# A spectral filter and a two-way maxout layer: filter loads in another order, and the first batch's input in fewer loads

## The chip, the cores and the metric

The kernel runs on one core of one Trainium2 chip. The metric is the device time of one execution in microseconds. A profile gives one execution's own span, from the first to the last instruction.

## The reference

```python
# x (8, 3072, 256), filt_r and filt_i (1537, 256); moe_w1 and moe_w2 (256, 1024), moe_w_out (1024, 256)
X = np.fft.rfft(x, axis=1)
Y = X * (filt_r + 1j * filt_i)[None, :, :]
y = np.fft.irfft(Y, n=3072, axis=1).astype(np.float32)
t = y.reshape(8 * 3072, 256)
out = np.maximum(t @ moe_w1, t @ moe_w2) @ moe_w_out
```

## The kernel before, in words

The transform of 3072 points is split into 96 by 32 points, and both steps and their inverses are matrix products on TensorE with bf16 tables of sines and cosines that the kernel makes at its start. The eight batches (indices 0 to 7) go through four steps one after another: a first transform over 96 points, a transform over 32 points (`s2`), the product with the filter (`product`, line 393), and the way back (`s3`, `s4`). The maxout layer works on 64 blocks of 384 tokens. Its matmuls (lines 453 and 481) make up most of the run, and an order written out by hand puts the transforms of batch b + 1 and b + 2 between the matmuls of batch b. Nothing of that can start before batch 0 has gone through its transforms, and batch 0 has code of its own: `s1t`, `t1`, `s2`, `products`, `s3t`, `t2`, in which the intermediate results stay on the core.

**What the start loads.** The program for GpSimd's queue begins with eight loads of x for batch 0, `load_x(0, c, 1)` for c from 0 to 7, with small index tables (`iota`) between the first ones. Each takes a chunk of 4 rows for each of 96 partitions, and the DMA turns float32 into bf16. `s1t(c)` on TensorE (line 507) transforms chunk c. Before it, 12 matmuls with no use for the result (`spin`, line 567) keep TensorE busy. Behind the x loads stand 18 loads of the filter.

**The filter's layout.** The filter tile `F` has 128 partitions, `[128, 2, 12, 2, 256]`: the second index `ri` is filt_r or filt_i, the third is `w` from 0 to 11. A load fills 16 partitions. Partitions fall into two array halves `g` (0 to 63 and 64 to 127). In each half, partitions 0 to 15 hold frequencies in rising order (the plus sign, line 121, one run of rows), partitions 16 to 31 hold frequencies in falling order (the minus sign, line 124, row by row backwards), and partitions 32 to 63 are a copy of the first 32. Where `g` is 0 and `w` starts at 0, the minus sign needs one more small load (line 127). `load_f(h, sign)` loads w 0 to 7 for h = 0 and w 8 to 11 for h = 1. So h = 0 has ten loads and h = 1 has eight.

**The copies.** `double_f(h, g, ri, engine)` copies partitions 0 to 31 of a half to 32 to 63, for four values of `w`. For w 4 to 7 (its h = 1) and 8 to 11 (h = 2) it is a DMA on SyncE's queue (line 136), eight in all; for w 0 to 3 (h = 0) it is a copy on VectorE (line 134). Each waits for the plus and the minus loads of its own `g` and `ri`. On SyncE, four loads of the layer's weights (lines 289 and 290) stand behind the eight copies.

**Who waits for the filter.** `products(v)` for v from 0 to 5 needs w 2v and 2v + 1 of both halves and of both `ri`: v 0 and 1 need VectorE's copies, v 2 and 3 SyncE's first four, v 4 and 5 its last four. For v below 4 one of its two products is on GpSimd, and all others are on VectorE. `s3t(v)` (lines 532 and 538) follows on TensorE.

**Semaphores.** The framework gives the DMAs of GpSimd's queue eight completion semaphores in turn. A DMA whose semaphore is still in use by the DMA eight places before it is issued only when that one has landed, and the queue behind it waits too.

Of the kernel before, what the change touches and what calls it, by code (L numbers as in the profile page):

```python
# [15 lines left out]
D = 256  # L16
# [10 lines left out]
def kernel(  # L27
# [15 lines left out]
    V, S, G, TE = nc.vector, nc.scalar, nc.gpsimd, nc.tensor  # L43
# [7 lines left out]
    F = const.tile([128, 2, NW, 2, D], BF16)  # L51
# [26 lines left out]
    def x_tile(b, c):  # L78
        if c % 2 == 0:
            xb[b] = xpool.tile([128, 8, D], BF16, tag="xb", name="xb")  # L80
        return xb[b][:, 4 * (c % 2):4 * (c % 2) + 4]

    def load_x(b, c, n):
        for k in range(c, c + n):
            xb[b, k] = x_tile(b, k)[0:NP]
        src = x[b].rearrange("(p m) d -> p m d", m=NM)
        m0 = 4 * (c % 2)
        G.dma_start(out=xb[b][0:NP, m0:m0 + 4 * n], in_=src[:, 4 * c:4 * c + 4 * n, :])  # L88
# [18 lines left out]

    WP = ((0, 8), (8, 12))

    def load_f(h, sign):  # L110
        w0, w1 = WP[h]
        n = 2 * (w1 - w0)
        for g in range(2):
            for ri, f in enumerate((filt_r, filt_i)):
                k0 = 24 * g + 2 * w0
                n0 = 1 if k0 == 0 else 0
                r0 = 64 * g if sign > 0 else 64 * g + 16
                o_ = F[r0:r0 + 16, ri, w0:w1].rearrange("p w s d -> p (w s) d")
                if sign > 0:
                    src = bass.AP(f.tensor, f.offset + k0 * D, [[96 * D, 16], [D, n], [1, D]])  # L120
                    G.dma_start(out=o_, in_=src)
                else:
                    src = bass.AP(f.tensor, f.offset + (96 - k0 - n0) * D, [[96 * D, 16], [-D, n - n0], [1, D]])
                    G.dma_start(out=o_[:, n0:n], in_=src)
                    if n0:
                        src = bass.AP(f.tensor, f.offset + 48 * D, [[96 * D, 16], [1, D]])
                        G.dma_start(out=o_[:, 0], in_=src)


    def double_f(h, g, ri, engine):  # L130
        ws = slice(4 * h, 4 * h + 4)
        o_, i_ = F[64 * g + 32:64 * g + 64, ri, ws], F[64 * g:64 * g + 32, ri, ws]
        if engine is V:
            V.tensor_copy(o_, i_)
        else:
            nc.sync.dma_start(out=o_, in_=i_)
# [3 lines left out]
    def load_fn():  # L140
        nc.sync.dma_start(out=FN[32:33], in_=filt_r[1536:1537, :])

    def fix_f():
        V.tensor_copy(F[32:33, 0, 0, 0], FN[32:33])
# [5 lines left out]
    def one(name):  # L150
# [11 lines left out]

    hv = init.tile([128, 2, 64], FP32)
    U0 = init.tile([128, 2, 64], BF16)
    load_x(0, 0, 1)
    G.iota(pid, pattern=[[1, 1]], base=0, channel_multiplier=1, allow_small_or_imprecise_dtypes=True)
    G.iota(kc.rearrange("p v g i s -> p v g (i s)"), pattern=[[4, 6], [24, 2], [1, 4]], base=0, channel_multiplier=0,
           allow_small_or_imprecise_dtypes=True)
    load_x(0, 1, 1)
    G.iota(kap, pattern=[[4, 6], [24, 2], [2, 2]], base=0, channel_multiplier=0,  # L170
           allow_small_or_imprecise_dtypes=True)
    G.iota(jb, pattern=[[1, 16]], base=0, channel_multiplier=0, allow_small_or_imprecise_dtypes=True)
    load_x(0, 2, 1)
    G.iota(cid, pattern=[[1, 128]], base=0, channel_multiplier=0, allow_small_or_imprecise_dtypes=True)
    for c in range(3, 8):
        load_x(0, c, 1)
    G.memset(hv, 1.0)
    for q in range(2):
        G.memset(hv[0:64, q, 0:64:32], 0.5 * (1 - q))
    for h in range(2):  # L180
        load_f(h, 1)
        load_f(h, -1)
    load_fn()

    def table_c():
# [329 lines left out]
    def t1(n, engine):  # L515
        pb = single.tile([128, 4, D], BF16, tag="single", name="pb")
        for i in range(4):
            for dc in range(2):
                TE.transpose(pb[:, i, 128 * dc:128 * dc + 128],
                             at2[:, dc, 4 * n + i].rearrange("p q m -> p (q m)"), I128)  # L520
        if engine is S:
            S.activation(bt[0][:, 4 * n:4 * n + 4], pb, AF.Copy)
        else:
            V.tensor_copy(bt[0][:, 4 * n:4 * n + 4], pb)
# [48 lines left out]
    V.tensor_scalar(NI, cid, pid, -1.0, OP.is_equal, OP.mult)  # L573
    tables_u()
    for h in (1, 2):
        for g in range(2):
            for ri in range(2):
                double_f(h, g, ri, nc.sync)
    for h in range(2):
        load_w(h)  # L580
# [10 lines left out]
    sines_u(1)  # L591
    for n in range(6):
        t1(n, S if n % 2 else V)
    for g in range(2):
        for ri in range(2):
            double_f(0, g, ri, V)
            if g == 0 and ri == 0:
                fix_f()
# [100 lines left out]
    for tt in range(8 * B + 1):  # L699
        b, i = divmod(tt, 8)  # L700
        k = 0
        for j in range(8):
# [5 lines left out]
            if tt > 0:  # L708
                n = 3 if j in (3, 7) else 4
# [36 lines left out]
```

## Time and profile before

| | us |
|---|---|
| median of 3 runs | 511.97 |
| lowest and highest run | 509.62, 512.15 |
| profiled execution, own time | 510.68 |
| its span | 508.9 |
| TensorE busy in the span | 492.5 (97%) |
| VectorE, ScalarE, GpSimd busy | 329.6, 307.6, 253.7 |

The profile's page groups instructions by line of the kernel; its other views are the chain of work that ended last, the timeline of one engine, sums over stretches of time, and the DMA issues with their time to landing. PE is TensorE, DVE VectorE, ACT ScalarE, POOL GpSimd, SP SyncE. A row of GpSimd's or SyncE's timeline named DMA_DIRECT2D is the issue of a transfer, not the transfer.

### The profile page before, as it was taken

The page shows a single profiled execution, that of the slowest core. Times are in us where ns is not written, and L with a number is a line of the kernel's source. Part 1 is how long each engine was busy: PE and PEld are TensorE (multiplying, and loading weights), DVE is VectorE, ACT ScalarE, POOL GpSimd, SP SyncE. Part 2 cuts the span into 40 slices and gives each one's busy share as a digit, 9 for nine tenths or more (in the row PEclk, how much of TensorE's full clock was granted, in tenths as well). Part 3 has the DMA queues.
Part 4 walks back from the last instruction along what each step waited for, and adds up shares of the span by engine and source line. Part 5 has one row for each costly group of instructions (what it writes and reads, how often), then busy time and mean ns, then how long its engine had stood idle before and what let it go on. Part 6 is the DMA issues. An engine that isn't in the chain of part 4 may idle for free.

```text
span 508.9 us, 13067 instructions
## 1 busy us (share of the span) xinstructions
PE 492.5 (97%) x5302; PEld 364.7 (72%) x5302; DVE 329.6 (65%) x517; ACT 307.6 (60%) x612; POOL 253.7 (50%) x334
## 2 busy tenths in 40 slices
PE   8679999999999999999999999999999999999996
PEld 4445777777777777777777777777777777777775
DVE  7655579656874677557774677657774687554453
ACT  6745558746784576646774576646774465544442
POOL 7783159674845566538636556538642221222220
PEclk9957999999999999999999999999999999999999
DMA  8998697999699778795689768797769326411112
GB/s 134 149 255 160 187 258 234 275 271 237 221 256 263 186 219 234 233 258 174 194 227 266 196 211 221 217 254 179 219 177 244 99 105 166 166 63 64 63 63 83
DMA packets 78158, 97.72 MB, mean 192 GB/s; under 512 B 8081, under 2 KB 54418, under 8 KB 78034
## 3 DMA queue, kind: packets, MB, share of 16 engines
q1 hardware_dynamic: 64834, 67.26, 50.3%
q0 software_dynamic: 13264, 29.64, 21.0%
q8 instruction: 41, 0.67, 0.6%
q14 instruction: 19, 0.16, 0.1%
HBM read 53.87 MB, written 47.19 MB: 199 GB/s over the span
## 4 chain that ended last, share of the span: by engine, by line
PE 90%; DMA 5%; DVE 2%; POOL 1%; issue 0%; SPq 0%; ACT 0%; DVEq 0%; POOLq 0%
PE po L481 34%; PE ph L453 32%; PE po L479 8%; PE pz L404 5%; PE py L433 4%; DMA F<-in_filt_r_dram 3%; PE pa L357 2%; PE px L387 2%; DMA xb<-in_x_dram 1%; DMA F<-F 1%; PE pr L557 1%; PE pz L538 1%; DVE at L335 0%; DVE pq L393 0%; PE pa L332 0%; POOL xb L88 0%
## 5 line engine op out<-in xcount | busy, mean ns | idle before, releaser
L481 PE MATMUL po<-Wo,gt 128*128 128x256 bf16 x1536 | 261.0, 273 | 0.0
L457 ACT ACTIVATE gt<-ph 128x384 bf16<-128x384 f32 x321 | 157.0, 496 | 148.1 <-PE ph L453 147.5
L481 PEld LDWEIGHTS <-gt 128*128 128x128 bf16 x1536 | 146.7, 98 | 65.7 <-issue 9.9
L466 POOL DMA_DIRECT2D out_dram<-ot x186 | 102.4, 555 | 179.5 <-DVE ot L493 176.7
L455 DVE TENSOR_SCALAR gt<-ph 128x384 bf16<-128x384 f32 x191 | 105.0, 553 | 62.9 <-PE ph L453 61.0
L393 DVE TENSOR_TENSOR pq<-px,F 128x1024 bf16<-128x1024 f32 x92 | 108.3, 1219 | 28.5 <-PE px L387 22.6
L453 PEld LDWEIGHTS <-Wd 128*128 128x128 bf16 x1024 | 96.6, 98 | 11.9 <-issue 0.5
L103 POOL TENSOR_TENSOR xb<-XF 128x512 bf16<-128x512 f32 x48 | 61.2, 1276 | 50.6 <-DMA XF<-in_x_dram 35.1
L493 DVE COPY ot<-po 128x512 f32<-128x512 f32 x95 | 65.2, 686 | 25.2 <-PE po L481 21.1
L104 POOL TENSOR_TENSOR xb<-XF 128x512 bf16<-128x512 f32 x48 | 61.0, 1272 | 0.0
L408 ACT ACTIVATE zt<-pz 128x512 bf16<-128x512 f32 x84 | 45.6, 595 | 11.5 <-PE pz L404 9.2
L361 ACT ACTIVATE at<-pa 128x512 bf16<-128x512 f32 x96 | 51.8, 610 | 1.2 <-PE pa L357 0.8
L433 PE MATMUL py<-G,zr 96*128 96x96 bf16 x512 | 32.9, 207 | 0.1
L433 PEld LDWEIGHTS <-zr 96*128 96x128 bf16 x512 | 29.3, 98 | 2.7 <-DVE zr L560 0.8
L387 PE MATMUL px<-bt,U 64*64 64x256 bf16 x384 | 20.6, 280 | 3.1 <-DVE pq L393 1.8
L404 PE MATMUL pz<-pq,VP 64*64 64x256 bf16 x336 | 21.9, 281 | 0.0
L404 PE MATMUL pz<-pq,VQ 64*64 64x256 bf16 x336 | 20.9, 269 | 0.0
L357 PE MATMUL pa<-xb,CT 64*64 64x512 bf16 x192 | 19.5, 383 | 0.0
L404 PEld LDWEIGHTS <-VP 64*64 64x64 bf16 x336 | 9.7, 105 | 13.3 <-issue 13.3
L387 PEld LDWEIGHTS <-U 64*64 64x64 bf16 x384 | 10.4, 108 | 6.6 <-issue 6.3
L567 PE MATMUL pd<-W 128*128 128x512 bf16 x31 | 12.0, 507 | 1.5 <-DVE zero L156 1.5
L560 DVE COPY zr<-pr 96x1024 bf16<-96x1024 bf16 (+1 forms) x8 | 5.2, 649 | 8.7 <-PE pr L557 8.7
(428 smaller groups left out, 607.6 us busy)
## 6 DMA issues: line engine op xcount, KB each, us to landing
out_dram<-ot POOLq DMA_DIRECT2D x186, 128.0 KB, 3.5
XF<-in_x_dram SPq DMA_DIRECT2D x96, 192.0 KB, 4.8
ad<-at SPq DMA_DIRECT2D x56, 192.0 KB, 3.2
bt<-ad SPq DMA_DIRECT2D x14, 768.0 KB, 9.2
zd<-zt SPq DMA_DIRECT2D x42, 256.0 KB, 2.4
zr<-zd SPq DMA_DIRECT2D x56, 192.0 KB, 4.8
WS<-in_moe_w_dram SPq DMA_DIRECT2D x4, 512.0 KB, 6.3
xb<-in_x_dram POOLq DMA_DIRECT2D x8, 192.0 KB, 5.3
```

What stands on the lines that cost most here:

```text
L103: G.tensor_tensor(t_[:, 0], f[:, 0], f[:, 1], OP.add)
L104: G.tensor_tensor(t_[:, 1], f[:, 0], f[:, 1], OP.subtract)
L361: S.activation(at[:, m0:m0 + 2], pa[g], AF.Copy)
L393: E.tensor_tensor(pq, px.rearrange("p (o i) d -> p o i d", o=1).to_broadcast([128, 2, 2, D]), F[:, :, 2 * v:2 * v + 2, s], OP.mult)
L404: TE.matmul(pz[g][64 * s:64 * s + 64, i], tab[64 * g:64 * g + 64, 2 * v + i, s], pq[s][64 * g:64 * g + 64, q, i], start=(q == 0), stop=(q ...
L433: TE.matmul(py[:, m], zr[b][:, 4 * i + m, 128 * dc:128 * dc + 128], G1, start=True, stop=True)
L453: TE.matmul(ph, Wd[:, dc, 128 * j:128 * j + 128], y_[:, dc], start=(dc == 0), stop=(dc == 1))
L455: V.tensor_scalar(gt[tt][:, j], ph, 0.0, None, OP.max)
L457: S.activation(gt[tt][:, j], ph, AF.Relu)
L466: E.dma_start(out=dst, in_=ot[tt // 2][:, 3 * (tt % 2) + c])
L481: TE.matmul(p_, g_[:, n - 2, blk], Wo[:, n - 2], start=(e == 0), stop=(e == 9))
L493: V.tensor_copy(ot[tt // 2][:, e - 1:e + 1], po[0])
```

## The change

Batch 0's x comes in five loads: three of two chunks each (0 and 1, 2 and 3, 4 and 5) and two of one chunk (6 and 7). `load_f` loses its argument `sign`. Within each h it now goes through `ri` first and then through `g`, and for each of these issues the plus load, the minus load and, where there is one, the small load, before it goes on. The numbers, sizes and places of the 18 filter loads are the same. The doubling copies go through `ri` outside and `g` inside, on SyncE and on VectorE.

```diff
-    def load_f(h, sign):
+    def load_f(h):
         w0, w1 = WP[h]
         n = 2 * (w1 - w0)
-        for g in range(2):
-            for ri, f in enumerate((filt_r, filt_i)):
+        for ri, f in enumerate((filt_r, filt_i)):
+            for g in range(2):
                 k0 = 24 * g + 2 * w0
+                src = bass.AP(f.tensor, f.offset + k0 * D, [[96 * D, 16], [D, n], [1, D]])
+                G.dma_start(out=F[64 * g:64 * g + 16, ri, w0:w1].rearrange("p w s d -> p (w s) d"), in_=src)
                 n0 = 1 if k0 == 0 else 0
-                r0 = 64 * g if sign > 0 else 64 * g + 16
-                o_ = F[r0:r0 + 16, ri, w0:w1].rearrange("p w s d -> p (w s) d")
-                if sign > 0:
-                    src = bass.AP(f.tensor, f.offset + k0 * D, [[96 * D, 16], [D, n], [1, D]])
-                    G.dma_start(out=o_, in_=src)
-                else:
-                    src = bass.AP(f.tensor, f.offset + (96 - k0 - n0) * D, [[96 * D, 16], [-D, n - n0], [1, D]])
-                    G.dma_start(out=o_[:, n0:n], in_=src)
-                    if n0:
-                        src = bass.AP(f.tensor, f.offset + 48 * D, [[96 * D, 16], [1, D]])
-                        G.dma_start(out=o_[:, 0], in_=src)
+                src = bass.AP(f.tensor, f.offset + (96 - k0 - n0) * D, [[96 * D, 16], [-D, n - n0], [1, D]])
+                G.dma_start(out=F[64 * g + 16:64 * g + 32, ri, w0:w1].rearrange("p w s d -> p (w s) d")[:, n0:n],
+                            in_=src)
+                if n0:
+                    src = bass.AP(f.tensor, f.offset + 48 * D, [[96 * D, 16], [1, D]])
+                    G.dma_start(out=F[16:32, ri, 0, 0], in_=src)
...
-    load_x(0, 0, 1)
+    load_x(0, 0, 2)
...
-    load_x(0, 1, 1)
+    load_x(0, 2, 2)
...
-    load_x(0, 2, 1)
+    load_x(0, 4, 2)
...
-    for c in range(3, 8):
+    for c in range(6, 8):
         load_x(0, c, 1)
...
     for h in range(2):
-        load_f(h, 1)
-        load_f(h, -1)
+        load_f(h)
...
     for h in (1, 2):
-        for g in range(2):
-            for ri in range(2):
+        for ri in range(2):
+            for g in range(2):
                 double_f(h, g, ri, nc.sync)
...
-    for g in range(2):
-        for ri in range(2):
+    for ri in range(2):
+        for g in range(2):
             double_f(0, g, ri, V)
             if g == 0 and ri == 0:
                 fix_f()
```

## The prediction

> **What bounds the kernel now.** I read the page first. TensorE is busy for 492.5 of 508.9 us, so little is left for any change that does not touch the matmuls, and what is left lies at the start.
>
> ```profile
> span 508.9 us, 13067 instructions
> ...
> PE 492.5 (97%) x5302; PEld 364.7 (72%) x5302; DVE 329.6 (65%) x517; ACT 307.6 (60%) x612; POOL 253.7 (50%) x334
> ```
>
> Then the chain of work that ended last, because it tells what the first 40 us wait for. Columns: start, length, what.
>
> ```profile
> 10.70 8.31 DMA F<-in_filt_r_dram
> ...
> 20.71 5.75 DMA F<-in_filt_r_dram
> ...
> 26.52 0.51 SPq L136
> ...
> 28.41 4.86 DMA F<-F
> ...
> 33.69 2.37 DVE pq L393 x2
> ...
> 40.76 0.66 PE pa L332
> ```
>
> The chain runs through filter loads and not through TensorE until the product at 33.69: a filter load lands at 10.70 + 8.31 = 19.0, another at 26.46, then SyncE issues the last four doubling copies one behind the other, the last at 28.41; it lands 4.86 later, at 33.27, and that product starts on VectorE. From 40.76 on the chain is matmuls. So the filter's path sets when the long part starts, and a microsecond on it is a microsecond of the whole.
>
> Third, GpSimd's timeline, which issues these loads (start, length, what; in brackets the idle time before it and who ended it).
>
> ```profile
> 1.28 0.67 POOL L88 DMA_DIRECT2D xb<-in_x_dram  x1 [0.83 <-POOLq L730]
> ...
> 4.11 2.53 POOL L88 DMA_DIRECT2D xb<-in_x_dram  x5
> ...
> 7.15 0.50 POOL L121 DMA_DIRECT2D F<-in_filt_r_dram  x1
> ...
> 9.22 0.48 POOL L121 DMA_DIRECT2D F<-in_filt_i_dram  x1 [0.50 <-DMA xb<-in_x_dram]
> 10.70 0.58 POOL L124 DMA_DIRECT2D F<-in_filt_r_dram  x1 [0.99 <-DMA xb<-in_x_dram]
> 11.64 0.69 POOL L127 DMA_DIRECT2D F<-in_filt_r_dram  x1 [0.36 <-DMA xb<-in_x_dram]
> 12.61 0.59 POOL L124 DMA_DIRECT2D F<-in_filt_i_dram  x1 [0.29 <-DMA xb<-in_x_dram]
> 14.51 0.50 POOL L127 DMA_DIRECT2D F<-in_filt_i_dram  x1 [1.30 <-DMA xb<-in_x_dram]
> 15.30 0.58 POOL L124 DMA_DIRECT2D F<-in_filt_r_dram  x1 [0.30 <-DMA F<-in_filt_r_dram]
> 16.24 0.56 POOL L124 DMA_DIRECT2D F<-in_filt_i_dram  x1 [0.36 <-DMA F<-in_filt_i_dram]
> ...
> 22.69 0.59 POOL L124 DMA_DIRECT2D F<-in_filt_i_dram  x1
> ```
>
> The built program gives GpSimd's DMAs eight semaphores in turn, so each issue waits until the DMA eight before it has landed. That is what the brackets show: filter loads 4 to 8 are let go by x loads 4 to 8, load 9 by filter load 1, load 10 by load 2, and so on to load 18, which waits for load 10. Load 1 was issued at 7.15 but had landed only just before 15.30, some 0.8 us after the last x load (14.51): it stood behind x.
>
> Load 10, issued at 16.24, took
>
> ```profile
> DMA to landing us min/median/max: 6.2/6.2/6.2
> ```
>
> and landed at 22.4. It is the hinge: it completes the first half of the filter, so the last of the three copies on VectorE and the last doubling of that half wait for it, and load 18 (the row at 22.69; its group's row below has 5.1 us to landing) is issued 0.3 us behind it.
>
> ```profile
> 21.08 2.07 DVE L134 COPY F<-F 32x2048 bf16<-32x2048 bf16 x3 [0.62 <-DMA F<-in_filt_i_dram]
> 23.26 2.35 DVE L393 TENSOR_TENSOR pq<-px,F 128x1024 bf16<-128x1024 f32 x2
> ```
>
> ```profile
> F<-in_filt_i_dram POOLq DMA_DIRECT2D x4, 64.0 KB, 5.1
> ```
>
> **The change part by part.**
>
> *Three x loads fewer.* An issue takes 2.53/5 = 0.51 us of GpSimd, so three fewer bring the first filter load from 7.15 to about 5.6 us. With five x loads instead of eight, filter loads 1 to 3 need no release, load 4 waits for the first pair, load 5 for the second, and load 6 for the third pair, which ends with the same x chunk that released it before (11.64). From load 6 on every issue hangs on the same landing as before. Since load 1 stood behind x anyway, the earlier issue of loads 1 to 5 gives nothing: 0.
>
> *The x transfers themselves.* The bytes are the same. The releases at 9.22, 10.70, 11.64, 12.61 and 14.51 stand for x loads 4 to 8 and are 1.48, 0.94, 0.97 and 1.90 us apart. If pairs did away with what is over 0.95, the last x load would land 0.53 + 0.95, about 1.5 us earlier, and the filter loads queued behind it too. If the excess belongs to the DMA engines and not to the number of loads, 0. It is not below nothing for the path: a pair lands as a whole, which could hold back the transforms of its first chunk, but these are covered twice.
>
> ```profile
> 6.56 0.63 PE L507 MATMUL pa<-C,xb 96*128 96x96 bf16 x8
> ...
> 14.28 0.51 PE L507 MATMUL pa<-C,xb 96*128 96x96 bf16 x8 [0.95 <-DMA xb<-in_x_dram]
> ```
>
> The first transform starts at 6.56 behind warm-up matmuls, and a pair issued at 25.38 with little beside it landed after
>
> ```profile
> DMA to landing us min/median/max: 5.1/5.1/5.1
> ```
>
> so the first pair should be there at 1.28 + 5.1 = 6.4. The last transform (14.28) waits for the last x load, which stays single. If that cover is gone, the price is a transform of 0.6 us. I take 0.4 us off the hinge here, nearer to 0, since two of the four spacings show no excess.
>
> *The order of the filter loads.* Load 10 is the minus-sign load of filt_i for g = 1 in both orders, with the same nine loads ahead of it; its own queue does not bring it sooner. What differs is what comes between. Before, the first doubling copy could start only at 19.1, when the first minus-sign load had landed.
>
> ```profile
> 19.09 9.87 SPq L136 DMA_DIRECT2D F<-F  x8
> ```
>
> Now the first doubling needs loads 1 and 2, there at about 16.2, and the second loads 4 and 5, there at 19.0 as load 5 was. So two doublings of 128 KB enter a stretch in which the queue is full.
>
> ```profile
> 16.00:20.00 4.00, 3.48 (x99) 2.95 (x99) 2.61 (x4) 3.47 (x5) 2.27 (x4) 1.00 1.90 132
> 20.00:25.00 5.00, 1.91 (x88) 1.23 (x88) 4.16 (x7) 3.18 (x5) 4.72 (x7) 0.89 1.12 164
> 40.00:45.00 5.00, 4.25 (x24) 2.60 (x25) 1.67 (x3) 2.25 (x4) 1.34 (x1) 0.56 1.27 208
> ```
>
> (The last three columns are granted clock, DMA share and GB/s.) At 164 GB/s a doubling is 0.8 us of all DMA engines. Both in full ahead of load 10 would be +1.6 us; none, if they fill gaps, 0. The share of 1.90 between 16 and 20 us leaves few gaps, but the second doubling comes when load 10 is half through; I take +0.5. [...]
>
> So the hinge moves by -0.4 + 0.5 = +0.1 us, to 22.5. The copies on VectorE change order, but the last still waits for load 10, so the product at 23.26 stays within 0.1 us.
>
> *The end of the filter path.* Load 18 is issued 0.3 us after load 10, at 22.8, and lands 5.1 us later, at 27.9. Before, it landed at 22.69 + 5.1 = 27.8, but the loads of all four second-half doublings came in together from 26.46, and SyncE, which needs some 0.63 us for each (26.52 to 28.41 are three steps), issued the last one at 28.41. Now the loads come in by pairs, the first three doublings are out before load 18 lands, and the last is issued right behind it, at 27.9. That is 28.41 - 27.8 = -0.6 us before the hinge's +0.1, and what follows (4.86 us of transfer, then the product) is unchanged. VectorE can take it: it sat idle for 3.6 us before that product.
>
> ```profile
> DVE pq L393 <- DMA F<-F: 5.7, 2, 3.6
> ```
>
> SyncE's weight loads behind the doublings move with them. Nothing after 45 us changes its order on any engine.
>
> Sum: -0.4 + 0.5 - 0.6 = **-0.5 us**. The profiled execution took 510.68 us (508.9 of span, 1.8 around it) and would take 510.2; it lies 1.3 under the median of the runs shown, 511.97, so the forecast is **511.5 us**. The runs shown differ by 2.5 us, so that 0.5% (2.6 us) is about what a measurement of this kernel can tell from no change: this forecast is "no change".
>
> **The rivals.**
>
> *Faster: the pairs free the x phase (chance 0.30).* The whole excess of 1.5 us goes and the doublings fill gaps, so the hinge is at 20.9: -1.5 - 0.6 = -2.1 us. That alone is under 0.5%; the clock has to add to it. The granted clock is 0.56 from 40 to 45 us, while TensorE is busy for 4.25 of those 5 us; at full clock that work is 4.25 x 0.56 = 2.4 us, so an earlier return is worth up to 1.8 us. The case is a gain of -2.6 to -3.9 us, taken at -3.2: 508.8. For it: two long spacings among the x landings; against it: two spacings show no excess, and the clock has to help. [...]
>
> *Slower: the doublings hold up the filter (chance 0.20).* Three doublings, not two, get in front of load 10 or of the second-half loads: 3 x 0.8 = 2.4 us, so the hinge is at 24.8. With the 0.6 us from SyncE taken off, +1.8, and if the half clock stays longer, another 1.8 at most. The case is +2.6 to +3.6, taken at +3.1: 515.1. It decides when load 10 lands after about 24 us and the clock also returns later, or after 25.6 (22.4 + 0.6 + 2.6) alone. For it: the share of 1.90; against it: the third doubling needs loads 6 and 7, which land late.
>
> *The order does nothing (inside the forecast's 0.50).* If SyncE's issue at the end still bunches, because loads 12 to 18 land together, the 0.6 us is not gained either: +0.1 us.
>
> **How the numbers follow.** The forecast has 0.50, its bounds being -0.6 - 1.5 and -0.6 + 1.6 around it: 509.9 to 513.0. Both other cases are reached into: the low end of 508.0 takes in the faster case down to -3.9, and the high end of 514.8 cuts the slower one (514.6 to 515.6) short, so that some 2 in 10 are left out, most of them above. Faster by over 0.5% 0.30, within it 0.50, slower 0.20.
>
> **What would show it.** Filter loads 1 to 3 issued from 5.6 us without idle time; load 4 let go by the first pair; first doubling issued near 16 us instead of 19.1; load 10 landing at 22.5 (20.9 or 24.8 by the rivals); the last doubling issued within 0.1 us of load 18's landing, near 27.9; the late product at 33.2 instead of 33.69; the first batch-1 transform at 40.3. The forecast is wrong if load 10's landing moves by more than 1.5 us, if the last doubling does not follow load 18 at once, or if the granted clock returns in another window.

## The result, and the profile after

The changed kernel takes 507.43 us (median of 6 runs, 505.97 to 508.38) where the kernel before takes 511.52 on the same chip (6 runs, 509.62 to 512.15). The ratio is 0.9923, with a 95% interval of 0.9898 to 0.9947: faster by 0.8%, or 4.1 us. The forecast was 511.5 us and no change, and its range ended at 508.0. A second run of the changed kernel, `after_again`, gave 506.65 us and a ratio of 0.9912 (0.9888 to 0.9936). Of all executions below, one of `last_on_scalar` took 1006.26 us, twice the time of the other five, and is left out of its ratio, not of its median.

The profiled execution of the changed kernel took 508.38 us with a span of 506.6. It is the slowest of its six runs, so this trace shows 2.3 of the 4.1 us. The chain of work that ended last, of the changed kernel (start, length, what):

```profile
span 506.6 us, 13064 instructions
...
5.88 10.19 DMA F<-in_filt_r_dram
...
16.36 0.57 POOL F L120
...
20.78 5.48 DMA F<-in_filt_i_dram
...
26.31 6.14 DMA F<-F
...
32.87 2.37 DVE pq L389 x2
...
39.65 0.43 PE pa L328
...
42.28 0.61 PE ph L449 x2
```

The kinds of links are those of before: filter loads, the last doubling copy, the late product, the batch-1 transform. Three things are new. Right ahead of the last copy stands load 18 (the row at 20.78), where before it was load 15 (the prediction's row at 20.71) and four issues of SyncE. From 16.36 to 20.78 the chain runs through GpSimd's own issues (it has POOL rows there, of about half a microsecond each), because loads 11 to 18 no longer wait for landings: their rows from 16.93 to 20.78 have no idle time before them, where before load 11 waited 0.52 us, load 12 0.42 and load 13 0.55 for a landing. And the half clock ends earlier. The same stretches as in the prediction, with one row of before for the stretch not shown there (last three columns: granted clock, DMA share, GB/s). Changed kernel:

```profile
16.00:20.00 4.00, 3.58 (x57) 3.04 (x58) 2.90 (x5) 3.57 (x5) 3.67 (x8) 1.00 0.89 149
...
25.00:40.00 15.00, 9.50 (x222) 5.76 (x217) 7.87 (x8) 6.62 (x8) 11.57 (x10) 0.67 0.94 241
40.00:45.00 5.00, 4.92 (x42) 2.89 (x41) 2.83 (x6) 2.76 (x5) 3.01 (x4) 1.00 1.17 186
```

Kernel before:

```profile
25.00:40.00 15.00, 11.57 (x265) 6.89 (x262) 7.59 (x7) 6.47 (x8) 12.00 (x10) 0.50 1.00 254
```

Between 16 and 20 us the DMA engines moved more (149 against 132 GB/s) with less than half the busy share (0.89 against 1.90). The share adds up the times of the packets, over the span of the 16 engines, so at 1.90 packets overlap in time in an engine. Since less was moved at 1.90 than at 0.89, a part of that time is presumably waiting; no view shows how much. After 25 us the granted clock is 0.67 instead of 0.50, and it is full from 40 us, where it was 0.56.

All of the difference lies ahead of the layer. Its first matmul (`ph`) starts at 42.28, and 506.6 - 42.3 is 464.3. In the kernel before it starts here, and 508.9 - 44.6 is 464.3 as well:

```profile
44.61 0.62 PE L453 MATMUL ph<-y__957,Wd 128*128 128x384 bf16 x2
```

GpSimd's timeline of the changed kernel answers the steps on the loads:

```profile
5.40 0.50 POOL L117 DMA_DIRECT2D F<-in_filt_r_dram  x1
5.88 0.60 POOL L120 DMA_DIRECT2D F<-in_filt_r_dram  x1
...
9.80 0.57 POOL L120 DMA_DIRECT2D F<-in_filt_r_dram  x1 [2.33 <-DMA xb<-in_x_dram]
11.70 0.54 POOL L117 DMA_DIRECT2D F<-in_filt_i_dram  x1 [1.34 <-DMA xb<-in_x_dram]
...
16.36 0.57 POOL L120 DMA_DIRECT2D F<-in_filt_i_dram  x1 [0.33 <-DMA F<-in_filt_r_dram]
16.93 0.48 POOL L117 DMA_DIRECT2D F<-in_filt_r_dram  x1
```

The row at 16.36 is load 10, the hinge. Its time to landing:

```profile
DMA to landing us min/median/max: 4.0/4.0/4.0
```

It was issued 0.1 us later than before (16.24) and landed at 20.3 instead of 22.4. What of this is due to the order, and what to x, this trace alone can't tell.

### The profile page after: what moved, and what is told of

Its sections match the earlier page's. It is cut to its first block, busy times and chain, and to the rows that moved or that the text cites. A ratio compares the mean times of both kernels' runs of the same rounds, so it can differ in the third digit from the quotient of the medians.

```text
span 506.6 us, 13064 instructions
## 1 busy us (share of the span) xinstructions
PE 489.4 (97%) x5302; PEld 363.1 (72%) x5302; DVE 329.7 (65%) x517; ACT 307.4 (61%) x612; POOL 251.7 (50%) x331
## 4 chain that ended last, share of the span: by engine, by line
PE 90%; DMA 4%; DVE 2%; POOL 2%; ACT 1%; issue 0%; DVEq 0%; POOLq 0%; ACTq 0%; SPq 0%
PE po L477 34%; PE ph L449 33%; PE po L475 8%; PE pz L400 5%; PE py L429 4%; PE pa L353 2%; DMA F<-in_filt_r_dram 2%; PE px L383 2%; DMA F<-F 1%; DMA F<-in_filt_i_dram 1%; PE pr L553 1%; POOL F L120 0%; PE pz L534 0%; POOL xb L88 0%; DVE at L331 0%; DVE pq L389 0%
## 5 line engine op out<-in xcount | busy, mean ns | idle before, releaser
L400 PE MATMUL pz<-pq,VQ 64*64 64x256 bf16 x336 | 20.9, 269 | 0.0
L563 PE MATMUL pd<-W 128*128 128x512 bf16 x31 | 10.8, 466 | 1.5 <-DVE zero L153 1.5
```

The source lines that it names most:

```text
L400: TE.matmul(pz[g][64 * s:64 * s + 64, i], tab[64 * g:64 * g + 64, 2 * v + i, s], pq[s][64 * g:64 * g + 64, q, i], start=(q == 0), stop=(q ...
```

## The experiments

Where a time to landing or an issue is given without a row, it is read from the DMA issues and their landings in that kernel's trace. All ratios are to the kernel before on the same chip, whose median stands beside each; runs on different chips are compared by their ratios.

### Each half of the change alone

`x5_only` has the five x loads and the old order:

```diff
-    load_x(0, 0, 1)
+    load_x(0, 0, 2)
...
-    for c in range(3, 8):
+    for c in range(6, 8):
```

> Only the five x loads; filter loads and copies in the old order. A: no gain, 0.998 to 1.002 of the kernel before, filter load 10 lands within 0.5 us of 22.4. B: most of the gain, 0.993 to 0.995, load 10 lands near 20.5. What the prediction took: -0.4 us.

`order_only` has the new `load_f` and the new order of copies, with eight x loads. Its diff is the change's without the lines on `load_x`.

> Only the new order of the filter loads and of the copies; x in eight loads. A: 0.992 to 0.994 of the kernel before, load 10 lands near 20.5, the last doubling is issued right behind load 18. B: at most the 0.6 us of the last doubling, 0.998 to 1.000. What the prediction took: -0.1 us (+0.5 for doublings in the way, -0.6 at the end).

> The changed kernel, beside the parts of the change on the same chip. Theory A (order: the alternation of plus and minus loads lets the DMA engines work through the first ten filter loads in 5.9 us behind x instead of 8.2 us): 0.992 of the kernel before. Theory B (five x loads free the semaphores, so four filter loads are queued by 7 us): the same. [...]

> The kernel before, a second trace. If the 8.2 us from the landing of the last x load to the landing of filter load 10 belong to the old order, they show again (7.5 to 8.5); if they were an accident of one execution, some 6 us.

| | median us | before there | ratio (95%) | load 10 landed | last copy issued | late product |
|---|---|---|---|---|---|---|
| before | 511.52 | | | 22.41 | 28.41 | 33.69 |
| `before_again` | 510.74 (one run) | 510.66 | | 21.87 | 27.78 | 34.07 |
| `x5_only` | 509.96 | 511.63 | 0.9967 (0.9947 to 0.9987) | 20.55 | 27.54 | 32.80 |
| `order_only` | 508.21 | 511.63 | 0.9932 (0.9907 to 0.9958) | 19.52 | 24.90 | 30.51 |
| changed kernel | 507.43 | 511.52 | 0.9923 (0.9898 to 0.9947) | 20.33 | 26.31 | 32.87 |
| `after_again` | 506.65 | 511.63 | 0.9912 (0.9888 to 0.9936) | | 24.39 | 30.74 |

The order of the filter loads alone gives 3.4 us, most of the gain, and the x loads alone 1.7. Together they give 4.1 and 5.0 us in the two runs, about the sum or a little less. `x5_only` fits neither of its theories whole: load 10 lands near 20.5, as theory B had it, but the gain is smaller than B's. Two traces of one kernel differ by up to 2 us in this stretch (the last two rows), so the medians carry the verdicts and the traces the mechanism.

Two marks that look telling do not separate the orders. From the landing of the last x load to that of load 10 it is 8.2 and 7.5 us in the two traces of before and 5.9 in the changed kernel's, but also 5.9 in `x5_only`, in the old order, and 8.5 in `held_copies` below, in the new one. And load 10 itself takes 6.2 us from issue to landing before, but 3.8 in `x5_only`, where it was issued at 16.79, and 6.1 in `held_copies`, where it was issued at 13.89. Load 18, the last one, is a better mark. It lands at 27.83 and 27.24 in the two traces of before, at 26.60 in `x5_only`, at 24.85 in `order_only`, at 26.26 in the changed kernel's trace, and in that of `after_again` ahead of 24.39, when the last copy goes out.

The DMA share doesn't separate the orders either. Between 16 and 20 us `x5_only`, in the old order, has a share below 1 and yet moves less than any other kernel of this table; `order_only`, with the eight x loads of before, moves 198 GB/s where before moved 132. `x5_only`, then `order_only`:

```profile
16.00:20.00 4.00, 3.48 (x65) 2.98 (x67) 3.04 (x5) 3.48 (x5) 3.34 (x7) 1.00 0.96 110
```

```profile
16.00:20.00 4.00, 3.48 (x122) 2.91 (x118) 3.49 (x6) 3.87 (x6) 3.95 (x7) 1.00 1.12 198
```

The chain of `order_only`:

```profile
20.08 4.77 DMA F<-in_filt_i_dram
24.90 5.19 DMA F<-F
...
30.51 2.37 DVE pq L389 x2
```

Load 18 (the first row) lands 3.0 us earlier than before, the last copy goes out 3.5 us earlier and the product starts 3.2 us earlier, near the median's 3.4.

### Which part of the order: sign, half, or pairs

`signs_only` takes the signs in turns but keeps `g` outside, and keeps the old order of copies. `halves_only` keeps the sign outermost and only swaps the loops, so that neighbouring loads go to the two array halves:

```diff
-        for g in range(2):
-            for ri, f in enumerate((filt_r, filt_i)):
+        for ri, f in enumerate((filt_r, filt_i)):
+            for g in range(2):
```

`late_pairs` puts only the last eight loads in plus and minus pairs, behind ten loads in the old order:

```diff
-    for h in range(2):
-        load_f(h, 1)
-        load_f(h, -1)
+    load_f(0, 1)
+    load_f(0, -1)
+    for g in range(2):
+        for ri in range(2):
+            load_f(1, 1, (g,), (ri,))
+            load_f(1, -1, (g,), (ri,))
```

> x in eight loads; plus and minus loads in turns, but array halves outside and filt_r, filt_i inside, with the copies in that old order too. A: like the whole new order, within 0.5 us of it. If the turn of halves and of filt_r and filt_i matters as well, it stays 1 us or more behind the whole new order. B: 0.998 to 1.000.

> Old order of signs (all plus loads of a part, then all minus loads), but array halves in turns (half inside, filt_r and filt_i outside); x in eight loads, copies in the old order. [...] Theory M (what matters is that large and small packets are mixed): nothing, 0.999 to 1.001.

> The old order for the first ten filter loads; only the last eight go in pairs of plus and minus, in the order in which SyncE's last four copies need them. The prediction's last step alone: -0.6 us, 0.999 of the kernel before, the last copy issued within 0.1 us of load 18's landing, load 10 where it was. If pairs also make the loads themselves faster, load 18 lands less than 5.1 us after its issue and the gain is 1 us or more.

| | median us | before there | ratio (95%) | load 10 landed | late product |
|---|---|---|---|---|---|
| `signs_only` | 507.68 | 511.63 | 0.9927 (0.9901 to 0.9952) | | 31.79 |
| `halves_only` | 508.78 | 510.66 | 0.9968 (0.9946 to 0.9990) | 19.69 | 31.59 |
| `late_pairs` | 510.19 | 510.66 | 0.9984 (0.9969 to 1.0000) | 20.91 | 33.58 |

Each alternation helps by itself, the sign by 3.7 us and the half by 1.6. In the old order the loads of filt_r and filt_i that follow each other fill the same 16 partitions. `signs_only` alternates by the sign and `halves_only` by the half, and both moved more between 16 and 20 us than the 132 GB/s of before, at a lower share than its 1.90. `signs_only`, then `halves_only`:

```profile
16.00:20.00 4.00, 3.32 (x117) 2.46 (x115) 3.67 (x6) 3.96 (x7) 3.64 (x7) 1.00 1.28 193
```

```profile
16.00:20.00 4.00, 3.48 (x124) 2.83 (x122) 3.05 (x6) 3.96 (x6) 3.17 (x6) 1.00 1.13 173
```

`signs_only` has the whole gain of `order_only` without the new order of copies, so that order gives nothing that could be measured. In the trace of `halves_only` load 18 lands at 25.54, 2.3 us earlier than before, but the last copy goes out only at 26.62: the loads of a copy do not come in pairs there, and the copies bunch at the end. `late_pairs` leaves the first ten loads in the old order and gets the staggered end: its last copy goes out at 27.79, right behind load 18's landing at 27.58. By its ratio it is worth 0.8 us, near the 0.6 forecast for that step, but its interval reaches 1, so a gain isn't shown.

### The loads by themselves

`load_bench` issues eight loads of 128 KB from GpSimd's queue one behind the other, with nothing beside them, to different places, waits until all have landed, and goes to the next list.

> No filter, no layer: thirteen stretches of eight filter loads of 128 KB each, to chosen partitions, with a wait between the stretches. Plus loads to partitions 0-15 alone (twice), to 0-15 and 32-47 in turns, 0-15 and 16-31, 0-15 and 64-79, all four of 0, 16, 64 and 80; the same for minus loads; then the old order of the kernel (plus 0, 0, 64, 64, minus 16, 16, 80, 80) and the new one (plus and minus, half by half). [...] Theory M: all plus stretches alike, all minus stretches alike, and only the last two differ.

In its GpSimd timeline each stretch begins with an issue and ends with a small copy that waited for the last landing. Plus loads: all to partitions 0 to 15; in turns to 0 and 32; in turns to 0 and 16; in turns to 0 and 64.

```profile
14.22 0.49 POOL L53 DMA_DIRECT2D T<-in_filt_r_dram  x1 [0.29 <-POOL d L73]
...
25.97 0.18 POOL L73 COPY d<-T 16x8 bf16<-16x8 bf16 x1 [7.93 <-DMA T<-in_filt_i_dram]
26.44 0.48 POOL L53 DMA_DIRECT2D T<-in_filt_r_dram  x1 [0.29 <-POOL d L73]
...
38.24 0.18 POOL L73 COPY d<-T 16x4 bf16<-16x4 bf16 x1 [0.56 <-DMA T<-in_filt_i_dram]
38.69 0.48 POOL L53 DMA_DIRECT2D T<-in_filt_r_dram  x1 [0.27 <-POOL d L73]
...
48.83 0.18 POOL L73 COPY d<-T 32x4 bf16<-32x4 bf16 x1 [6.33 <-DMA T<-in_filt_i_dram]
49.30 0.49 POOL L53 DMA_DIRECT2D T<-in_filt_r_dram  x1 [0.29 <-POOL d L73]
...
58.76 0.18 POOL L73 COPY d<-T 16x4 bf16<-16x4 bf16 x1 [0.31 <-DMA T<-in_filt_i_dram]
```

From issue to copy that is 11.75, 11.80, 10.14 and 9.46 us. Minus loads give 14.77, 14.40, 10.86 and 10.10 for the same four lists. The last two lists are the kernel's old order of its first eight large loads, and its new order:

```profile
133.80 0.50 POOL L53 DMA_DIRECT2D T<-in_filt_r_dram  x1 [0.29 <-POOL d L73]
...
145.69 0.18 POOL L73 COPY d<-T 32x2 bf16<-32x2 bf16 x1 [2.06 <-DMA T<-in_filt_i_dram]
146.16 0.50 POOL L53 DMA_DIRECT2D T<-in_filt_r_dram  x1 [0.29 <-POOL d L73]
...
156.18 0.18 POOL L73 COPY d<-T 32x2 bf16<-32x2 bf16 x1 [1.23 <-DMA T<-in_filt_i_dram]
```

11.89 against 10.02 us, so 1.9 us by the order alone, with no copies, no x and no compute beside it. What decides between these lists is not how many partitions a list touches but which: 0 and 32 are 32 partitions and took 11.80 us, as long as one place with 11.75, while 0 and 16 took 10.14 and 0 and 64 took 9.46. Minus loads fall into the same two groups (14.77 and 14.40 against 10.86 and 10.10). Mixing plus and minus loads isn't needed, since plus loads alone show it; by theory M all plus lists would be alike, and they are not.

The two quick pairs save 14 and 20% of the time of one place with plus loads (26 and 32% with minus loads), and four places in turns (0, 16, 64, 80) took 9.99 us with plus and 11.59 with minus loads, no quicker than 0 and 64. So it is shown that the places matter, and which pairs were quick; the reason isn't shown, and what holds the quick lists at some 9.5 to 10 us stays open. Each list ran once in one execution, but the one place with plus loads twice (12.50 us as the very first list).

### The x loads

Does the first filter load, issued 1.7 us sooner, make the gain of `x5_only`? `x5_late` adds six small fills on GpSimd ahead of it, so that it goes out at its old time:

```diff
-    G.memset(hv, 1.0)
+    for _ in range(7):
+        G.memset(hv, 1.0)
```

> The five x loads alone, as in x5_only, with six more memsets of the same small tile on GpSimd between them and the filter loads (0.26 us each), so that the first filter load is issued near 7.1 us as before. Theory Q (the gain of the five loads, 0.9967, is that filter loads stand in the queue earlier): the gain goes, 0.999 to 1.001. Theory X (pairs are worked through faster by most DMA engines): the gain stays, 0.995 to 0.998.

```profile
7.05 0.50 POOL L121 DMA_DIRECT2D F<-in_filt_r_dram  x1
```

509.97 us, ratio 0.9972 (0.9956 to 0.9989): as `x5_only`. The earlier issue gives nothing that could be measured, as the prediction had it, so what is left as its source is the transfers. Between 3 and 10 us the kernel before, then `x5_late`:

```profile
3.00:10.00 7.00, 7.00 (x50) 3.40 (x48) 5.98 (x32) 4.38 (x10) 5.93 (x17) 1.00 0.97 153
```

```profile
3.00:10.00 7.00, 6.58 (x41) 3.22 (x40) 5.98 (x32) 3.75 (x9) 6.16 (x20) 1.00 0.96 188
```

188 against 153 GB/s at the same busy share. `x_bench` moves the same 1.5 MB of x without the filter:

> No filter, no layer: six stretches, each loading one batch of x (1.5 MB as bf16): eight single loads twice, four pairs, three pairs and two single loads; then eight single loads and three pairs with two, with 14 VectorE operations beside them. If pairs are worked through faster by themselves: the third and fourth stretch are 1 us or more shorter than the second. [...]

```profile
13.98 4.03 POOL L58 DMA_DIRECT2D X<-in_x_dram  x8 [0.26 <-issue]
24.92 0.19 POOL L64 CAST d<-X 96x8 f32<-96x8 bf16 x1 [6.91 <-DMA X<-in_x_dram]
25.36 2.00 POOL L58 DMA_DIRECT2D X<-in_x_dram  x4 [0.26 <-issue]
36.08 0.19 POOL L64 CAST d<-X 96x8 f32<-96x8 bf16 x1 [8.72 <-DMA X<-in_x_dram]
36.53 2.52 POOL L58 DMA_DIRECT2D X<-in_x_dram  x5 [0.26 <-issue]
46.48 0.19 POOL L64 CAST d<-X 96x8 f32<-96x8 bf16 x1 [7.43 <-DMA X<-in_x_dram]
```

Eight singles take 10.94 us to the cast that waits for the last one, five loads 9.95, so 1.0 us less. The same two lists with 14 VectorE operations beside them take 11.17 and 10.24, so VectorE's work isn't what makes the difference. The landings tell where it lies: the eight singles come some 0.95 us apart but for one step of 1.56 us (2.05 beside VectorE), and pairs come 1.85 apart with no such step. That looks like the excess over 0.95 that the prediction saw. Four pairs take 10.72, which speaks against "fewer loads are quicker" as the whole reason; they lose 0.7 us at the first pair, which landed 5.00 us after its issue and 4.32 in the list of five. Why it did stays open, and so does what makes 1.0 us here 1.7 in the kernel: in the trace of `x5_only` the last x load lands no sooner than before (14.64 against 14.23), and yet load 10 lands 1.9 us sooner. Landings of x scatter much from trace to trace. With five x loads and the new order the last one landed at 14.41 in the changed kernel's trace, but between 11.4 and 12.7 in the traces of `after_again`, `after_warm`, `held_copies`, `copies_on_vector` and `last_on_scalar2`.

### Do the early copies hold up load 10?

`held_copies` is the changed kernel with SyncE's first four copies in reverse order, so that the first waits for the loads 9 and 10 and none comes ahead of load 10's landing:

```diff
-        for ri in range(2):
-            for g in range(2):
+        for ri in (range(2) if h == 2 else (1, 0)):
+            for g in (range(2) if h == 2 else (1, 0)):
```

> The changed kernel with SyncE's first four copies in the reverse order, so that none can start before filter load 10 has landed. If copies in the way of the loads cost what the prediction took (0.5 us at load 10) or more: load 10 lands earlier, but the four copies then go out one behind the other, 1.9 us; 0.992 to 0.994 of the kernel before. If they cost nothing: load 10 lands as in the changed kernel, the time is the same or up to 0.7 us longer, since the product of step 2 waits for the last of them.

```profile
20.05 5.65 SPq L133 DMA_DIRECT2D F<-F  x8
```

508.82 us, ratio 0.9961 (0.9941 to 0.9982). Load 10 lands at 19.96, against 20.33 in the changed kernel, though the last x load had landed 3.0 us sooner in this trace (11.41 against 14.41). So a cost of the early copies to load 10 is not seen: the two landings are 0.4 us apart, well within what two traces of a kernel differ by. By the ratios the kernel as a whole is 1.9 to 2.5 us slower than the changed one, more than the 0.7 expected: with the first copy at 20.05 the eight are issued back to back, and the last goes out 1.7 us behind load 18's landing (25.16 against 23.47). The bunching that the change removed is back, and would account for most of that.

`copies_on_vector` takes the last four copies off the DMA altogether:

```diff
-    for h in (1, 2):
-        for ri in range(2):
-            for g in range(2):
-                double_f(h, g, ri, nc.sync)
+    for ri in range(2):
+        for g in range(2):
+            double_f(1, g, ri, nc.sync)
...
+    for ri in range(2):
+        for g in range(2):
+            double_f(2, g, ri, V)
```

> The changed kernel with the last four doubling copies on VectorE instead of SyncE's DMAs, behind its fourth product. By the timeline of the changed kernel VectorE is idle from 28.2 to 32.9 us and a copy takes 0.69 us: the late product starts at 28.2 + 2.8 = 31.0 instead of 32.9, 1.9 us less than the changed kernel, 0.988 of the kernel before. Against it: SyncE's four weight loads are then issued near 21 us, beside the last filter loads, and may hold them up by 1 to 2 us; then no gain over the changed kernel.

517.24 us, ratio 1.0122 (1.0100 to 1.0143): slower. VectorE's timeline tells why.

```profile
26.25 13.95 DVE L131 COPY F<-F 32x2048 bf16<-32x2048 bf16 x4
40.30 4.62 DVE L389 TENSOR_TENSOR pq<-px,F 128x1024 bf16<-128x1024 f32 x4
```

Three of the four copies take 0.69 us as elsewhere, so the first one stands for 11.8 us, until 38.05; GpSimd is at work through nearly all of that time (busy for 9.98 of the 10 us from 25 to 35), and its work of this stretch ends at 38.9. The product comes at 40.30. It says nothing on the copies' DMA, but much on where not to put them.

### How much is the clock?

`before_warm` is the kernel before with more matmuls of no use where TensorE waited (six ahead of one table, and up to nine instead of one ahead of `s3t`), and `after_warm` is the changed kernel with the same:

```diff
-        TE.matmul(pz[0].rearrange("p i s r c m -> p (i s r c m)"), W1[:, 0:128], W1, start=True, stop=True)
+        for _ in range({1: 3, 2: 3, 4: 9, 3: 3}.get(v, 1)):
+            TE.matmul(pz[0].rearrange("p i s r c m -> p (i s r c m)"), W1[:, 0:128], W1, start=True, stop=True)
```

> The kernel before with more useless matmuls on TensorE where it waits for the filter (five more ahead of one table, two more each ahead of steps 1, 2 and 3, eight more ahead of step 4 of the way back), so that the clock is not cut or comes back sooner. If the clock's half rate costs nothing here: 1.000 to 1.004 (the extra matmuls). If it costs what the rows say (work of 40 to 45 us at 0.56): 0.996 to 0.998.

> The changed kernel with the same extra matmuls. Against before_warm: if the gain of the change is the filter's path alone, the two stand apart by as much as the kernels without them (4 to 5 us); if a part of the gain is the clock's return, by less (2 to 3 us), because the clock no longer differs.

```profile
25.00:40.00 15.00, 10.55 (x234) 5.74 (x234) 7.66 (x7) 6.39 (x8) 11.80 (x10) 1.00 0.92 233
```

That is `before_warm`: full clock where before had 0.50. It took 509.79 us, ratio 0.9970 (0.9953 to 0.9986), so the half clock costs the kernel before some 1.5 us. `after_warm` took 507.26, 0.9926 (0.9906 to 0.9946), the same as the changed kernel. Between the two warm kernels the change is worth 2.5 us. The trace of `after_warm` still shows 0.82 between 25 and 40 us, so the clock isn't quite taken out of that difference. By these medians some 1.5 of the 4.1 us came by the clock, and 2.5 or more by the filter path.

### The transfer of the last copy

In all these kernels the late product stands 5 to 7 us behind the last copy's issue. `last_on_scalar` is the changed kernel with that one copy on ScalarE:

```diff
-                double_f(h, g, ri, nc.sync)
+                if (h, ri, g) != (2, 1, 1):
+                    double_f(h, g, ri, nc.sync)
...
     s3t(0)
+    double_f(2, 1, 1, S)
```

> The changed kernel with one of the eight copies, the last one, on ScalarE behind its first evacuation of step 0 of the way back, instead of a DMA of SyncE. If the transfer time of that copy (4.9 to 6.1 us) ends the start, the late product follows load 18's landing by some 2 us (one copy of 2048 elements) instead of 6.6: 2 to 3 us less than the changed kernel, 0.986 to 0.988 of the kernel before. If ScalarE is held as VectorE was beside GpSimd's products: slower than the changed kernel.

> The changed kernel with the last copy of the filter (32 partitions, 4 KB each) on ScalarE instead of SyncE's transfer, for a profile to stand beside the earlier times. Theory (after load 18 has landed, the transfer of the last copy, 6.14 us in the changed kernel's profile, ends the start): time ratio 0.985 to 0.990 against the kernel before, the late product follows load 18's landing by under 3 us instead of 6.6, and the first batch-1 transform comes at 33 to 37 us. Rival (the late product has other waits that come due at the same time): the product comes no more than 1 us sooner than 30.7 us.

The first run gave 504.03 us, 0.9876 (0.9837 to 0.9914), the second 504.80, 0.9884 (0.9852 to 0.9916). This version beats both kernels, the changed one by 1.4 to 2.4 us going by the ratios, though the intervals overlap in part. The trace is that of the second run's fastest execution, while the changed kernel's is that of its slowest. ScalarE's timeline and then the chain:

```profile
25.69 1.91 ACT L133 ACTIVATE F<-F 32x2048 bf16<-32x2048 bf16 x1
```

```profile
22.81 4.97 DMA F<-F
...
27.90 4.63 DVE pq L391 x4
...
33.92 0.42 PE pa L330
```

Load 18 landed at 24.24 and ScalarE began the copy 1.45 us later, behind other work, for 1.91 us. The product started 3.7 us behind load 18 instead of 6.6 in the changed kernel's trace, and the batch-1 transform came at 33.92 instead of 39.65. It is not under 3 us because the copy before, still on SyncE, is now what ends last: issued at 22.81, it landed at 27.78. So the transfer of a copy did end the start, and it does so again with the next copy.

## Why the prediction was wrong

Point by point, in the order of its steps.

- **The place was right.** The whole gain that the traces show lies ahead of the first layer matmul, with 464.3 us behind it in both traces.
- **Three x loads fewer: right.** Filter loads 1 to 3 went out from 5.40 without idle time, load 4 too, since the first pair had landed by 5.9. Load 6 was let go at 11.70, for the 11.64 forecast. By `x5_late` the earlier issue is worth nothing that could be measured.
- **The x transfers: right in kind, too small.** 0.4 us was taken between 0 and 1.5; `x5_only` gives 1.7. In `x_bench` the excess over 0.95 us between landings is gone with pairs, as was argued, and worth 1.0; the rest of the 1.7 is unsettled.
- **The order of the filter loads: this step failed.** It reads "its own queue does not bring it sooner", with +0.5 us for the copies that come between and bounds of 0 to +1.6. Its hidden premise is that the same loads in the same queue take the same time in any order. They don't: with the next step's -0.6 the order should have come to -0.1, and it is worth -3.4 us (`order_only`); eight such loads by themselves take 1.9 us less (`load_bench`), and load 18 landed at 24.85 in `order_only` instead of 27.83. That loads to the same places delay each other (eight plus loads to one place 11.75 us, in turns to 0 and 64 9.46) was not a term of the sum. The row that could have warned was quoted: 132 GB/s between 16 and 20 us at a DMA share of 1.90. It was read as leaving "few gaps", but `order_only` moved 198 GB/s there.
- **The doublings in front of load 10: not seen.** In `held_copies`, without them, load 10 landed 0.4 us sooner, within the scatter of traces. The first doubling did go out near 16, at 16.16. That two doublings stand in full ahead of load 10, the bound of +1.6 us, no run here shows.
- **SyncE's last copy: right.** It was issued at 26.31, 0.05 us behind load 18, and `late_pairs`, at -0.8 where -0.6 was taken, is in line with it, though its interval reaches 1. Only the landing was wrong, 26.3 for 27.9.
- **What follows "is unchanged": not quite.** The last copy's transfer took 6.14 us in this trace instead of 4.86 and gave back 1.3 of the 2.1 us that it was issued sooner. In `order_only` it took 5.19.
- **The clock.** It did return in another window, earlier, as the faster rival had it: by the rows above it is 0.67 instead of 0.50 from 25 to 40 us, and 1.00 instead of 0.56 from 40 to 45. In this trace the product came 0.8 us sooner, the layer's first matmul 2.3 us sooner, so most of what it shows came by the clock; in the medians it is some 1.5 of 4.1.

The faster rival had the sign and nearly the size (508.8), and even its hinge near 20.9. It took all of its 1.5 us from x and left the order at nothing. The x loads alone do put load 10 at 20.55 (`x5_only`), but they are worth 1.7 us of the whole, and the order, which is worth twice that, is missing from it. So its near hit is in good part luck.

## What to carry to other kernels

The loads that stand behind one another in a queue were not exchangeable here. Each fills only 16 partitions, and eight of them took 10.14 and 9.46 us where neighbours went to places 16 or 64 partitions apart, but 11.75 and 11.80 where they went to the same ones or 32 apart (`load_bench`, plus loads); an order by places is worth a run. Low GB/s in a stretch in which loads are queued (132 before, 198 in `order_only`) is a sign to look at the order and the places of transfers before their number, whatever the DMA share beside it (1.90 at 132 GB/s before, 0.96 at 110 in `x5_only`). And judge by runs and by the landing of the last load, not by one load's time to landing. When a chain ends in a small DMA copy, an engine that is free at that moment is worth a try: the last copy took 4.86 us as a DMA before and 6.14 in the changed kernel, and 1.91 on ScalarE, but such a copy on VectorE beside a busy GpSimd took 11.8.

## What the runs showed of the hardware

A VectorE copy of 32 by 2048 bf16, 0.68 us elsewhere, took 11.8 us beside GpSimd's products and weight differences (`copies_on_vector`), while such a copy on ScalarE took 1.91 us (`last_on_scalar2`). VectorE's copy lasted over several instructions of GpSimd, whose longest single one here is 2.35 us; what held it isn't shown. Eight minus loads, whose rows run backwards and one by one, to one place of 16 partitions took 14.77 us where plus loads took 11.75; in turns to 0 and 64 it is 10.10 against 9.46, so in these lists the sign cost most where all go to one place (`load_bench`).
